# A fused causal conv and ELU MLP kernel: x loaded as fp32 and cast on chip, per-channel band weights, wide conv taps, w_out loaded earlier

## Chip, cores, metric

The kernel runs on one core of one Trainium2 chip. The metric is device time in microseconds (us), the median of a few executions. An execution of a one-core program counts as "fast" if it is within 1.5% of that kernel's fastest. A ratio is the mean time of one kernel's fast runs over the mean of the other's from the same rounds, so it is not quite the ratio of the medians that I quote.

The engines: PE is TensorE (matrix multiplies), DVE is VectorE, ACT is ScalarE, POOL is GpSimd, and SP is SyncE, which here only issues DMAs. DMAs that SP or ACT issue go through a hardware queue, those of GpSimd through the software queue. The granted clock is the share of its full speed at which PE is let run.

## The reference

```python
# x: (8, 4096, 192), weight: (8 heads, 7 taps), w_in: (192, 2048), w_out: (2048, 192)
w = softmax(weight, axis=-1)
out[b, s, h, :] = sum_k w[h, k] * x_pad[b, s + k, h, :]      # causal, 24 channels a head
h = out.reshape(32768, 192) @ w_in
g = where(h > 0, h, exp(min(h, 0)) - 1)
return g @ w_out                                             # float32
```

## The kernel before

The 32,768 tokens are handled in 32 super-tiles of 1,024. For each, a causal conv gives `att`, the first matmul with `w_in` gives 16 "pairs" of 2x512 columns in PSUM, ACT, POOL and DVE turn each pair into ELU values, and the matmuls with `w_out` follow one super-tile later. I number pairs from 0; pair 16 opens the second super-tile.

From the second super-tile on, the conv is a matmul with a banded matrix `Tm` that holds each head's 7 weights along a diagonal. `Tm` is made through DRAM by three DMAs that wait for each other: store zeros, write the diagonal over them, load the result. I call them the band chain: store, diagonal, reload.

```python
# SyncE (SP)
load_wd(sy, 0)                              # conv weights, one copy per channel
sy.dma_start(wq..., broadcast weight)       # all heads' weights on every partition
W(s_tz, 1); W(s_w[0], 32)                   # zeros ready; first part of w_in has landed
sy.dma_start(band[:, :, :], Tm[:, :, :]).then_inc(s_band, 16)          # store
W(s_band, 16); W(s_set, 5)                  # softmax of wq done
diagonal = bass.AP(tensor=band.tensor, offset=0,
                   ap=[[HEADS * TW + 1, P], [TW, HEADS], [1, KSIZE]])  # 128 x 8 x 7
sy.dma_start(diagonal, wprb[:]).then_inc(s_band, 16)                   # diagonal
W(s_band, 32)
sy.dma_start(Tm[:], band[:, :, :]).then_inc(s_band, 16)                # reload
```

The first super-tile cannot wait for that. Its conv uses x transposed on PE and small diagonal matrices `Dg` ("the early conv"), so that the w_in matmuls can start early. x comes as bf16 through GpSimd's software queue, which casts on the way; so do `w_in`, `w_out` and the later x tiles `xg`.

```python
# PE
warm(7)                                     # dummy matmuls of 512 columns
W(s_xl[0], 16); W(s_xl[1], 16)              # x has landed
# ... transposes, then 96 conv matmuls of 128 columns (48 pairs on two row groups)
# [cut] then in program order: pairs 0 to 6, banded conv, pairs 7 to 9, banded conv,
#       pairs 10 to 13, banded conv, pairs 14, 15, first w_out matmuls, pair 16 ...
if m == 0: W(s_band, 48)                    # the first banded conv waits for the band chain
elif n < NQ - 1: warm(2)                    # dummies between the first pairs
# GpSimd, ninth pair:  if n == W_OUT_AT (8): load w_out
```

Of the kernel before, what the change touches and what calls it, by code (L numbers as in the profile page):

```python
# [5 lines left out]
ALU = mybir.AluOpType  # L6
ACT = mybir.ActivationFunctionType
AXIS = mybir.AxisListType
# [21 lines left out]
LAG = -1  # L30
WCOLS = ((0, 512), (512, 1280), (1280, 2048))
Q_PART = (0,) * 4 + (1,) * 6 + (2,) * 6
WARM = (7, 2)
HALF_STEPS = (10, 10, 6, 6, 10, 11, 11)

CONV_AT = ((4, 1, 1), (12, 2, 0))
EARLY_CONV = {6: (1, 0), 9: (1, 1), 13: (2, 0)}
QUAD = 4
XTW = 136
HALO = 2  # L40
XW = 5
X_AT = ((5, 1), (10, 0), (13, 2))
W_OUT_AT = 8

PIECES = (
    ((0, 0, CW, 0), (1, 0, CW, CW), (2, 0, CW, 2 * CW), (3, 0, CW, 3 * CW), (4, 0, 24, 4 * CW)),
# [5 lines left out]
def bass_lightweight_conv__then__act_elu_kernel(  # L52
# [54 lines left out]
    for n in range(NP + NQ + LAG):  # L107
        s, i = divmod(n, NQ)
        if n < NP:
            slot_of_pair[n] = take_slot(("h", n))  # L110
            order.append(("h", n))
        if s == 0:
            convs = [EARLY_CONV[n]] if n in EARLY_CONV else []
        else:
            convs = [(s + ahead, g) for at, ahead, g in CONV_AT if at == i and n < NP]
        convs = [(k, g) for k, g in convs if k < NS]
        if n in rounds_at:
            t, half, r0, r1 = rounds_at[n]
            if (t, half) == last_half and r0 == 0:
                last_slot = take_slot(None)  # L120
            mid = (r0 + r1) // 2 if convs else r1
            order.append(("o", t, half, r0, mid))
            for k, g in convs:
                conv_at(k, g)
            if mid < r1:
                order.append(("o", t, half, mid, r1))
        else:
            for k, g in convs:
                conv_at(k, g)
# [5 lines left out]
    with ExitStack() as stack:  # L135
        def sbuf(name, shape, dt):
            return stack.enter_context(nc.sbuf_tensor(name, shape, dt))
# [4 lines left out]
        def sema(name):  # L142
            return stack.enter_context(nc.semaphore(name))
# [18 lines left out]
        E = sbuf("E", [P, NE, 2, GS], FP32)  # L162
        gT = sbuf("gT", [P, NG3, NQ, 2, GS], FP16)
        osb = sbuf("osb", [P, 2, 2, 2, D], FP32)
        wq = sbuf("wq", [P, HEADS, KSIZE], FP32)
        wmx = sbuf("wmx", [P, HEADS], FP32)
        wq2 = sbuf("wq2", [P, HEADS, KSIZE], FP32)
        wex = sbuf("wex", [P, HEADS, KSIZE], FP32)
        wsum = sbuf("wsum", [P, HEADS], FP32)
        wrs = sbuf("wrs", [P, HEADS], FP32)  # L170
        wprb = sbuf("wprb", [P, HEADS, KSIZE], BF16)
        zw = sbuf("zw", [P, GS], BF16)
        scr = sbuf("scr", [P, 2], FP32)
        H = psum("H", [P, 3, 2 * GS])
        ops = psum("ops", [P, 2, GS])

        s_wq = sema("s_wq")
        s_w = [sema(f"s_w{i}") for i in range(4)]
        s_wd = sema("s_wd")
        s_xl = [sema(f"s_xl{i}") for i in range(2)]  # L180
        s_id = sema("s_id")
        s_one = sema("s_one")
        s_z0 = sema("s_z0")
# [6 lines left out]
        s_hc = sema("s_hc")  # L190
        s_ha = sema("s_ha")
        s_hd = sema("s_hd")
        s_set = sema("s_set")
        s_wex = sema("s_wex")
        s_scr = sema("s_scr")
        s_x = [[sema(f"s_x{i}_{g}") for g in range(2)] for i in range(NXB)]
        s_od = sema("s_od")
# [86 lines left out]
        def _gpsimd(g: bass.BassGpSimd):  # L284
# [24 lines left out]
            def load_w_in(k):  # L309
                c0, c1 = WCOLS[k]  # L310
                for r in range(2):
                    g.dma_start(  # L312
                        w_in[HP * r : HP * (r + 1), :, c0:c1],
                        moe_w_in.rearrange("(p j) f -> p j f", j=3)[:, :, c0:c1],
                    ).then_inc(s_w[k], 16)

            def load_head(k):
                g.dma_start(
                    xh[:, k, :, :].rearrange("p i d -> p (i d)"),
                    x_flat[GS * k : GS * (k + 1), :].rearrange("(p i) d -> p (i d)", i=QUAD),  # L320
                ).then_inc(s_xl[k], 16)

            load_head(0)
            load_head(1)
            W(s_one, 1)
            g.affine_select(
                out=ident[:],
# [9 lines left out]
            for part in (1, 2):  # L337
                load_x(1, part)
            load_w_in(2)
            for n in range(NP):  # L340
                s, i = divmod(n, NQ)
                if n == W_OUT_AT:
                    g.dma_start(
                        w_out[:, :, :], moe_w_out.rearrange("(q p) d -> p q d", p=FC)
                    ).then_inc(s_w[3], 16)
                for at, part in X_AT:
                    if at == i and s + NXB < NS:
                        load_x(s + NXB, part)
                for u in range(2):
                    W(s_exp, 2 * n + u + 1)  # L350
                    g.tensor_scalar(  # L351
                        out=E[:, n % NE, u, :],
                        in0=E[:, n % NE, u, :],
                        scalar1=1.0,
                        scalar2=0.0,
                        op0=ALU.min,
                        op1=ALU.max,
                    ).then_inc(s_clp)

        @block.scalar  # L360
        def _scalar(a):
            W = Waits(a)
            load_wd(a, 1)
            a.memzero(scr[:, 0:1]).then_inc(s_scr)
            W(s_scr, 1)
            a.activation(scr[:, 1:2], scr[:, 0:1], ACT.Exp)
            W(s_v, 3)
            a.activation(wde[:], wd2[:], ACT.Exp, accum_out=wds[:]).then_inc(s_de)
            W(s_tp, 1)
# [16 lines left out]
            a.activation(  # L386
                att[:, 0, 2, 0 : GS // 2], H[:, 0, 0 : GS // 2], ACT.Copy
            ).then_inc(s_ha)
            W(s_set, 2)
            a.activation(wex[:], wq2[:], ACT.Exp).then_inc(s_wex)  # L390
            def evac(t, half):
                n_half = 2 * t + half
                W(s_mm2, n_half + 1)
# [42 lines left out]
        def _vector(v):  # L436
# [11 lines left out]
            v.tensor_scalar(  # L448
                out=wd2[:], in0=wd[:], scalar1=wdm[:, 0:1], scalar2=None, op0=ALU.subtract
            ).then_inc(s_v)  # L450
            W(s_de, 1)
            v.reciprocal(wdr[:], wds[:]).then_inc(s_v)
            W(s_v, 4)
# [5 lines left out]
                op0=ALU.mult,  # L459
                op1=ALU.mult,  # L460
            ).then_inc(s_D)
            W(s_tp, 3)
            v.tensor_copy(xT[:, 1, :, HALO : HALO + P], xt_bank(1)).then_inc(s_xtd)  # L463
            W(s_hc, 2)
# [1 line left out]
                att[:, 0, 1, :].rearrange("p (r t) -> p r t", r=2),  # L466
                H[:, 2, :].rearrange("p (r t) -> p r t", r=2)[:, :, 0 : GS // 2],
            ).then_inc(s_hd)
            W(s_wq, 16)
            v.tensor_reduce(wmx[:], wq[:], AXIS.X, ALU.max).then_inc(s_set)  # L470
            W(s_hc, 3)
            v.tensor_copy(
                att[:, 0, 2, GS // 2 : GS], H[:, 0, GS : GS + GS // 2]
            ).then_inc(s_hd)
            W(s_set, 1)
            v.tensor_tensor(
                wq2[:],
                wq[:],
                wmx[:, :].unsqueeze(2).to_broadcast([P, HEADS, KSIZE]),
                ALU.subtract,  # L480
            ).then_inc(s_set)
            W(s_wex, 1)
            v.tensor_reduce(wsum[:], wex[:], AXIS.X, ALU.add).then_inc(s_set)
            W(s_set, 3)
            v.reciprocal(wrs[:], wsum[:]).then_inc(s_set)
            W(s_set, 4)
            v.tensor_tensor(
                wprb[:, :, ::-1],
                wex[:],
                wrs[:, :].unsqueeze(2).to_broadcast([P, HEADS, KSIZE]),  # L490
                ALU.mult,
            ).then_inc(s_set)
            for n in range(NP):
                s, q = divmod(n, NQ)
                if s >= NG3:
# [20 lines left out]
        def _tensor(pe):  # L516
# [24 lines left out]

            warm(WARM[0])
            W(s_id, 1)
            W(s_xl[0], 16)
            W(s_xl[1], 16)
            for j in range(3):
                for i in range(QUAD):
                    ins = pe.matmul(  # L548
# [22 lines left out]
            for j in range(3):  # L571
                W(s_xta, (2, 2, 3)[j])
                if j:
                    W(s_xtd, 1)
                for k in range(KSIZE + 1):
                    for kb in range(2):
                        shift, i = divmod(2 * kb - PAD + k, QUAD)
                        for r in range(2):
                            ins = pe.matmul(  # L579
                                head_bank(j, r)[:, P * kb : P * (kb + 1)],  # L580
                                Dg[HP * r : HP * (r + 1), k : k + 2, :],
                                xT[HP * r : HP * (r + 1), j, i, HALO + shift : HALO + shift + P],
                                start=(k == 0 and kb == 0),
                                stop=(k == KSIZE),
                                tile_position=(HP * r, 0),
                                skip_group_check=True,
                            )
                ins.then_inc(s_hc)
            for item in order:
                if item[0] == "c":  # L590
# [79 lines left out]
        @block.sync  # L670
        def _sync(sy):
            W = Waits(sy)
            load_wd(sy, 0)
            sy.dma_start(
                wq[:, :, :].rearrange("p h k -> p (h k)"),
                bass.AP(tensor=weight.tensor, offset=0, ap=[[0, P], [1, HEADS * KSIZE]]),
            ).then_inc(s_wq, 16)
            W(s_tz, 1)
            W(s_w[0], 32)
            sy.dma_start(band[:, :, :], Tm[:, :, :]).then_inc(s_band, 16)  # L680
            W(s_band, 16)
            W(s_set, 5)
            diagonal = bass.AP(
                tensor=band.tensor,
                offset=0,
                ap=[[HEADS * TW + 1, P], [TW, HEADS], [1, KSIZE]],
            )
            sy.dma_start(diagonal, wprb[:]).then_inc(s_band, 16)
            W(s_band, 32)
            sy.dma_start(Tm[:], band[:, :, :]).then_inc(s_band, 16)  # L690

# [54 lines left out]
```

## Time and profile before

| | before |
|---|---|
| median | 759.63 us (758.85 to 760.06, 4 runs) |
| span of the profiled execution | 758.2 us |
| w_in matmuls begin (pair 0) | 15.42 us |
| first banded conv begins | 24.21 us |
| second super-tile begins (pair 16) | 43.27 us |

The windows view gives each engine's busy time in a stretch ("0.00:50.00 50.00" is the stretch and its length; PEclk is the granted clock).

```profile
core 0: us, PE busy (x) PEld busy (x) DVE busy (x) ACT busy (x) POOL busy (x), PEclk, DMA share, GB/s
0.00:50.00 50.00, 39.04 (x536) 19.32 (x539) 30.01 (x58) 29.69 (x56) 33.56 (x58) 1.00 0.69 114
50.00:100.00 50.00, 50.00 (x968) 35.04 (x958) 42.69 (x71) 44.72 (x80) 44.94 (x76) 1.00 0.45 96
```

From 50 us on PE is never free (further windows show the same up to 730 us); the only room is the head, the part before. So the start of pair 16 is the figure to follow: whatever moves it moves the end. The timeline of before (start, duration, engine, line, operation, and in brackets the idle time before it and what ended it):

```profile
8.42 0.61 PE L548 MATMUL H<-ident,xh 128*64 128x2 bf16 x9 [4.00 <-DMA xh<-in_x_dram]
...
10.83 0.34 SPq L680 DMA_DIRECT2D conv_band<-Tm  x1
...
15.42 0.82 PE L628 MATMUL H<-att,w_in 64*128 64x512 bf16 x6 [0.57 <-ACT att L386]
...
17.58 0.38 SPq L688 DMA_DIRECT2D conv_band<-wprb  x1
...
21.13 0.33 SPq L690 DMA_DIRECT2D Tm<-conv_band  x1
...
24.21 0.65 PE L604 MATMUL H<-Tm,xg 128*24 128x122 bf16 x40 [0.21 <-DVE gT L499]
...
43.27 0.82 PE L628 MATMUL H<-att,w_in 64*128 64x512 bf16 x6 [1.30 <-DMA att<-conv_slots]
```

A step of the band chain is issued when the one before it has landed, so the SPq lines give the chain's times: store 10.8 to 17.5, diagonal 17.6 to 21.1, reload 21.1 to about 24. The first conv waited for nothing of note: the band came just in time. Pair 16 waited 1.30 us for `att`.

### The profile page before, as it was taken

How to read it: one execution, taken by the hardware profiler on the slowest of the kernel's cores; microseconds unless marked ns; L12 is line 12 of the kernel's file. 1: busy time of each engine (PE TensorE's matmuls, PEld its weight loads, DVE VectorE, ACT ScalarE, POOL GpSimd, SP SyncE). 2: the span in 40 equal slices, each digit the busy share in tenths (PEclk: the TensorE clock that was granted, in tenths of full speed). 3: DMA queues.
4: the chain of work that ended last, by engine and by line, in shares of the span. 5: the costliest groups of instructions: out<-in, count | busy, mean ns of one | idle time of the engine just before them, and what ended most of it. 6: DMA issues, size and time to landing. Idle time of an engine off the chain costs nothing.

```text
span 758.2 us, 32332 instructions
## 1 busy us (share of the span) xinstructions
PE 742.6 (98%) x13911; PEld 513.4 (68%) x13911; DVE 636.8 (84%) x1043; ACT 646.9 (85%) x1161; POOL 660.6 (87%) x1107
## 2 busy tenths in 40 slices
PE   6889999999999999999999999999999999999997
PEld 4256676676767667667667667667667667667676
DVE  3778988988988988988988988988988988988993
ACT  3778888888888888888888888888888889889882
POOL 4879989989988988988988998988988998988892
PEclk9999999999999999999999999999999999999999
DMA  9643453443453453453453454354354354354112
GB/s 144 108 84 94 102 114 77 104 103 85 101 116 77 100 111 80 100 116 81 96 108 87 95 116 87 90 116 82 92 116 95 82 116 86 89 115 104 61 44 64
DMA packets 107135, 72.77 MB, mean 96 GB/s; under 512 B 44784, under 2 KB 106736, under 8 KB 106992
## 3 DMA queue, kind: packets, MB, share of 16 engines
q1 hardware_dynamic: 66344, 54.03, 23.6%
q0 software_dynamic: 40304, 16.47, 19.7%
q8 instruction: 109, 1.79, 1.0%
q14 instruction: 34, 0.28, 0.1%
q10 hardware_dynamic: 344, 0.20, 0.1%
HBM read 45.43 MB, written 41.71 MB: 115 GB/s over the span
## 4 chain that ended last, share of the span: by engine, by line
PE 95%; DMA 2%; ACT 1%; DVE 1%; POOL 1%; issue 0%; SPq 0%; POOLq 0%
PE H L628 44%; PE ops L657 44%; PE H L604 5%; DMA conv_slots<-csb 1%; DMA xh<-in_x_dram 1%; PE H L657 1%; DVE gT L499 0%; DMA att<-conv_slots 0%; PE ops L531 0%; ACT E L427 0%; PE H L579 0%; POOL E L351 0%; PE ops L579 0%; PE H L560 0%; SPq L279 0%
## 5 line engine op out<-in xcount | busy, mean ns | idle before, releaser
L499 DVE SCALAR_TENSOR_TENSOR gT<-E,H 128x512 f16<-128x512 f32 x1024 | 631.0, 682 | 98.4 <-POOL E L351 90.9
L351 POOL TENSOR_SCALAR E<-E 128x512 f32<-128x512 f32 x1024 | 604.0, 612 | 82.9 <-ACT E L427 79.3
L427 ACT ACTIVATE E<-H 128x512 f32<-128x512 f32 x1024 | 546.2, 605 | 87.4 <-PE H L628 73.8
L657 PEld LDWEIGHTS ops<-w_out,gT 64*128 64x128 f16 x8064 | 342.4, 94 | 109.6 <-ACT osb L405 10.9
L657 PE MATMUL ops<-w_out,gT 64*128 64x192 f16 x8064 | 414.4, 243 | 0.9 <-DVE gT L499 0.9
L628 PE MATMUL H<-att,w_in 64*128 64x512 bf16 x3072 | 407.3, 378 | 5.1 <-DVE gT L499 3.2
L628 PEld LDWEIGHTS H<-att,w_in 64*128 64x128 bf16 x3072 | 129.6, 94 | 107.2 <-DVE gT L499 6.0
L416 ACT ACTIVATE csb<-H 128x1024 bf16<-128x1024 f32 x62 | 63.5, 1024 | 0.0
L405 ACT ACTIVATE osb<-ops 128x768 f32<-128x768 f32 x63 | 51.6, 819 | 5.1 <-PE ops L657 5.1
L307 POOL DMA_DIRECT2D xg<-in_x_dram x62 | 52.2, 842 | 0.4 <-issue 0.4
L604 PE MATMUL H<-Tm,xg 128*24 128x122 bf16 (+1 forms) x2480 | 40.7, 209 | 0.7 <-DVE gT L499 0.7
L604 PEld LDWEIGHTS H<-Tm,xg 128*24 128x24 bf16 x2480 | 31.3, 92 | 11.3 <-issue 10.7
L531 PE MATMUL ops<-zw 128*128 128x512 bf16 x35 | 11.6, 434 | 1.2 <-DVE zw L438 1.2
L510 DVE COPY osb<-H 128x384 f32<-128x384 f32 x1 | 0.6, 558 | 8.9 <-PE H L657 8.9
L531 PEld LDWEIGHTS ops<-zw 128*128 128x128 bf16 x35 | 2.5, 106 | 7.5 <-issue 6.0
L657 PE MATMUL H<-w_out,gT 64*128 64x192 f16 x128 | 5.6, 243 | 0.1
L657 PEld LDWEIGHTS H<-w_out,gT 64*128 64x128 f16 x128 | 5.2, 94 | 0.3 <-PE H L657 0.3
L548 PE MATMUL H<-ident,xh 128*64 128x2 bf16 x12 | 0.8, 192 | 4.0 <-DMA xh<-in_x_dram 4.0
L397 ACT ACTIVATE osb<-H 128x384 f32<-128x384 f32 x1 | 0.5, 490 | 4.7 <-PE H L657 4.7
L548 PEld LDWEIGHTS H<-ident,xh 128*64 128x64 bf16 x12 | 0.7, 151 | 4.9 <-issue 4.9
L312 POOL DMA_DIRECT2D w_in<-in_moe_w_in_dram x6 | 3.8, 642 | 0.0
L463 DVE CAST xT<-H 128x512 bf16<-128x512 f32 x1 | 0.7, 692 | 3.5 <-PE H L560 3.5
(41 smaller groups left out, 26.4 us busy)
## 6 DMA issues: line engine op xcount, KB each, us to landing
out_dram<-osb SPq DMA_DIRECT2D x127, 192.0 KB, 2.7
conv_slots<-csb SPq DMA_DIRECT2D x62, 256.0 KB, 2.5
att<-conv_slots SPq DMA_DIRECT2D x186, 64.0 KB
xg<-in_x_dram POOLq DMA_DIRECT2D x31, 240.0 KB, 5.1
xg<-in_x_dram POOLq DMA_DIRECT2D x31, 192.0 KB, 4.4
w_in<-in_moe_w_in_dram POOLq DMA_DIRECT2D x4, 288.0 KB, 10.1
w_out<-in_moe_w_out_dram POOLq DMA_DIRECT2D x1, 768.0 KB, 9.9
xh<-in_x_dram POOLq DMA_DIRECT2D x2, 192.0 KB, 5.5
```

Of the source, the lines that this page charges most:

```text
L307: g.dma_start(xg[:, b, w0:w1, :], src).then_inc(s_x[b][part - 1], 16)
L312: g.dma_start(w_in[HP * r : HP * (r + 1), :, c0:c1], moe_w_in.rearrange("(p j) f -> p j f", j=3)[:, :, c0:c1],).then_inc(s_w[k], 16)
L351: g.tensor_scalar(out=E[:, n % NE, u, :], in0=E[:, n % NE, u, :], scalar1=1.0, scalar2=0.0, op0=ALU.min, op1=ALU.max,).then_inc(s_clp)
L405: a.activation(osb[:, b, :, :, :].rearrange("p g k d -> p g (k d)"), ops[:, :, 0 : 2 * D], ACT.Copy,).then_inc(s_oev)
L416: a.activation(csb[:, m % 4, :, :], H[:, slot_of_conv[m] % 3, :].rearrange("p (b t) -> p b t", b=2), ACT.Copy,).then_inc(s_ce)
L427: a.activation(E[:, n % NE, u, :], H[:, k, GS * u : GS * (u + 1)], ACT.Exp).then_inc(s_exp)
L499: v.scalar_tensor_tensor(out=gT[:, s % NG3, q, u, :], in0=E[:, n % NE, u, :], scalar=1.0, in1=H[:, slot_of_pair[n] % 3, GS * u : GS * (u + ...
L531: pe.matmul(ops[:, 0, :], zw[:, 0:P], zw[:], start=True, stop=True)
L548: ins = pe.matmul(halos()[HP:P, j, i, 0:HALO], xh[:, 0, i, j::3], ident[:, P - HALO : P], start=True, stop=True, tile_position=(0, HP),)
L604: ins = pe.matmul(H[SLOT * q : SLOT * q + CPH, k % 3, GS * hb + o : GS * hb + o + nc_], xg[:, s % NXB, w, CPH * h : CPH * (h + 1)], Tm[:, ...
L628: ins = pe.matmul(H[:, k % 3, GS * r : GS * (r + 1)], w_in[HP * r : HP * (r + 1), j, FC * q : FC * (q + 1)], att[HP * r : HP * (r + 1), s ...
L657: ins = pe.matmul(acc[:, g, D * kb : D * (kb + 1)], gT[HP * rt : HP * (rt + 1), t % NG3, q, g, t0 : t0 + P], w_out[HP * rt : HP * (rt + 1) ...
```

## The change

It is meant to start the head sooner. x arrives uncast through ACT's hardware queue and ACT and DVE cast it (both small loads of the conv weights now go out on SP; one was on ACT); eleven warm-ups instead of seven cover the wait; the early conv takes 256 columns at a time; the band's store waits for x only and its diagonal uses weights that exist per channel anyway; w_out is loaded at once; the third early banded conv moves behind pair 16.

```diff
-WARM = (7, 2)
+WARM = (11, 2)
-EARLY_CONV = {6: (1, 0), 9: (1, 1), 13: (2, 0)}
+EARLY_CONV = {6: (1, 0), 9: (1, 1), 16: (2, 0)}
 # GpSimd: the two casting loads of x are gone; w_out follows w_in directly
+            g.dma_start(w_out[:, :, :], ...)            # was: at the ninth pair
 # ACT: fp32 x in, half of it cast here
+            for k in range(2):
+                a.dma_start(xf[:, k, :, :]..., x_flat[GS * k : GS * (k + 1), :]...)
+            a.activation(xh[:, 0, :, :], xf[:, 0, :, :], ACT.Copy).then_inc(s_xha)
 # DVE: the other half, behind the per-channel softmax; the all-heads softmax is gone
             W(s_wd, 32)
             # ... max, subtract
+            W(s_xl[1], 16)
+            v.tensor_copy(xh[:, 1, :, :], xf[:, 1, :, :]).then_inc(s_xh)
+            v.tensor_scalar(out=wprb[:, ::-1], in0=wde[:], scalar1=wdr[:, 0:1], ...)
 # PE: 48 matmuls of 256 columns instead of 96 of 128   [cut]
 # SP
-            W(s_w[0], 32)
+            for r in range(2):
+                W(s_xl[r], 16)
             sy.dma_start(band[:, :, :], Tm[:, :, :]).then_inc(s_band, 16)
             W(s_band, 16)
-            sy.dma_start(diagonal, wprb[:])             # rows (128), heads (8), taps
+            W(s_wp, 1)
+            sy.dma_start(                               # heads (8), rows (128), taps
+                bass.AP(tensor=band.tensor, offset=0,
+                        ap=[[TW, HEADS], [HEADS * TW + 1, P], [1, KSIZE]]),
+                wprb[0:HP:8, :].unsqueeze(1).to_broadcast([HEADS, P, KSIZE]),
+            ).then_inc(s_band, 16)
```

More of the change, by code (lines that the diff above doesn't have):

```diff
@@ L42 @@
 X_AT = ((5, 1), (10, 0), (13, 2))
-W_OUT_AT = 8
 PIECES = (
@@ L111, in bass_lightweight_conv__then__act_elu_kernel @@
             order.append(("h", n))
-        if s == 0:
-            convs = [EARLY_CONV[n]] if n in EARLY_CONV else []
-        else:
-            convs = [(s + ahead, g) for at, ahead, g in CONV_AT if at == i and n < NP]
+        convs = [EARLY_CONV[n]] if n in EARLY_CONV else []
+        if s:
+            convs += [(s + ahead, g) for at, ahead, g in CONV_AT if at == i and n < NP]
         convs = [(k, g) for k, g in convs if k < NS]
@@ L164, in bass_lightweight_conv__then__act_elu_kernel @@
         osb = sbuf("osb", [P, 2, 2, 2, D], FP32)
-        wq = sbuf("wq", [P, HEADS, KSIZE], FP32)
-        wmx = sbuf("wmx", [P, HEADS], FP32)
-        wq2 = sbuf("wq2", [P, HEADS, KSIZE], FP32)
-        wex = sbuf("wex", [P, HEADS, KSIZE], FP32)
-        wsum = sbuf("wsum", [P, HEADS], FP32)
-        wrs = sbuf("wrs", [P, HEADS], FP32)
-        wprb = sbuf("wprb", [P, HEADS, KSIZE], BF16)
+        wprb = sbuf("wprb", [P, KSIZE], BF16)
+        xf = sbuf("xf", [P, 2, QUAD, D], FP32)
         zw = sbuf("zw", [P, GS], BF16)
@@ L175, in bass_lightweight_conv__then__act_elu_kernel @@
         ops = psum("ops", [P, 2, GS])
-        s_wq = sema("s_wq")
         s_w = [sema(f"s_w{i}") for i in range(4)]
@@ L180, in bass_lightweight_conv__then__act_elu_kernel @@
         s_xl = [sema(f"s_xl{i}") for i in range(2)]
+        s_xh = sema("s_xh")
+        s_xha = sema("s_xha")
+        s_wp = sema("s_wp")
         s_id = sema("s_id")
@@ L192, in bass_lightweight_conv__then__act_elu_kernel @@
         s_hd = sema("s_hd")
-        s_set = sema("s_set")
-        s_wex = sema("s_wex")
         s_scr = sema("s_scr")
@@ L315, in load_w_in @@
                     ).then_inc(s_w[k], 16)
-            def load_head(k):
-                g.dma_start(
-                    xh[:, k, :, :].rearrange("p i d -> p (i d)"),
-                    x_flat[GS * k : GS * (k + 1), :].rearrange("(p i) d -> p (i d)", i=QUAD),
-                ).then_inc(s_xl[k], 16)
-            load_head(0)
-            load_head(1)
             W(s_one, 1)
@@ L339, in _gpsimd @@
             load_w_in(2)
+            g.dma_start(
+                w_out[:, :, :], moe_w_out.rearrange("(q p) d -> p q d", p=FC)
+            ).then_inc(s_w[3], 16)
             for n in range(NP):
                 s, i = divmod(n, NQ)
-                if n == W_OUT_AT:
-                    g.dma_start(
-                        w_out[:, :, :], moe_w_out.rearrange("(q p) d -> p q d", p=FC)
-                    ).then_inc(s_w[3], 16)
                 for at, part in X_AT:
@@ L362, in _scalar @@
             W = Waits(a)
-            load_wd(a, 1)
+            for k in range(2):
+                a.dma_start(
+                    xf[:, k, :, :].rearrange("p i d -> p (i d)"),
+                    x_flat[GS * k : GS * (k + 1), :].rearrange("(p i) d -> p (i d)", i=QUAD),
+                ).then_inc(s_xl[k], 16)
             a.memzero(scr[:, 0:1]).then_inc(s_scr)
@@ L366, in _scalar @@
             a.activation(scr[:, 1:2], scr[:, 0:1], ACT.Exp)
+            W(s_xl[0], 16)
+            a.activation(xh[:, 0, :, :], xf[:, 0, :, :], ACT.Copy).then_inc(s_xha)
             W(s_v, 3)
@@ L388, in _scalar @@
             ).then_inc(s_ha)
-            W(s_set, 2)
-            a.activation(wex[:], wq2[:], ACT.Exp).then_inc(s_wex)
             def evac(t, half):
@@ L461, in _vector @@
             ).then_inc(s_D)
+            v.tensor_scalar(
+                out=wprb[:, ::-1], in0=wde[:], scalar1=wdr[:, 0:1], scalar2=None, op0=ALU.mult
+            ).then_inc(s_wp)
             W(s_tp, 3)
@@ L468, in _vector @@
             ).then_inc(s_hd)
-            W(s_wq, 16)
-            v.tensor_reduce(wmx[:], wq[:], AXIS.X, ALU.max).then_inc(s_set)
             W(s_hc, 3)
@@ L474, in _vector @@
             ).then_inc(s_hd)
-            W(s_set, 1)
-            v.tensor_tensor(
-                wq2[:],
-                wq[:],
-                wmx[:, :].unsqueeze(2).to_broadcast([P, HEADS, KSIZE]),
-                ALU.subtract,
-            ).then_inc(s_set)
-            W(s_wex, 1)
-            v.tensor_reduce(wsum[:], wex[:], AXIS.X, ALU.add).then_inc(s_set)
-            W(s_set, 3)
-            v.reciprocal(wrs[:], wsum[:]).then_inc(s_set)
-            W(s_set, 4)
-            v.tensor_tensor(
-                wprb[:, :, ::-1],
-                wex[:],
-                wrs[:, :].unsqueeze(2).to_broadcast([P, HEADS, KSIZE]),
-                ALU.mult,
-            ).then_inc(s_set)
             for n in range(NP):
@@ L543, in _tensor @@
             W(s_id, 1)
-            W(s_xl[0], 16)
-            W(s_xl[1], 16)
+            W(s_xha, 1)
+            W(s_xh, 1)
             for j in range(3):
@@ L575, in _tensor @@
                 for k in range(KSIZE + 1):
-                    for kb in range(2):
-                        shift, i = divmod(2 * kb - PAD + k, QUAD)
-                        for r in range(2):
-                            ins = pe.matmul(
-                                head_bank(j, r)[:, P * kb : P * (kb + 1)],
-                                Dg[HP * r : HP * (r + 1), k : k + 2, :],
-                                xT[HP * r : HP * (r + 1), j, i, HALO + shift : HALO + shift + P],
-                                start=(k == 0 and kb == 0),
-                                stop=(k == KSIZE),
-                                tile_position=(HP * r, 0),
-                                skip_group_check=True,
-                            )
+                    shift, i = divmod(k - PAD, QUAD)
+                    step = 2 * XTW if i < 2 else 1 - 2 * XTW
+                    for r in range(2):
+                        whole = xT[HP * r : HP * (r + 1), j, i, HALO + shift : HALO + shift + P]
+                        ins = pe.matmul(
+                            head_bank(j, r),
+                            Dg[HP * r : HP * (r + 1), k : k + 2, :],
+                            bass.AP(
+                                tensor=whole.tensor,
+                                offset=whole.offset,
+                                ap=[whole.ap[0], [step, 2], [1, P]],
+                            ),
+                            start=(k == 0),
+                            stop=(k == KSIZE),
+                            tile_position=(HP * r, 0),
+                        )
                 ins.then_inc(s_hc)
@@ L672, in _sync @@
             W = Waits(sy)
-            load_wd(sy, 0)
-            sy.dma_start(
-                wq[:, :, :].rearrange("p h k -> p (h k)"),
-                bass.AP(tensor=weight.tensor, offset=0, ap=[[0, P], [1, HEADS * KSIZE]]),
-            ).then_inc(s_wq, 16)
+            for r in range(2):
+                load_wd(sy, r)
             W(s_tz, 1)
-            W(s_w[0], 32)
+            for r in range(2):
+                W(s_xl[r], 16)
             sy.dma_start(band[:, :, :], Tm[:, :, :]).then_inc(s_band, 16)
             W(s_band, 16)
-            W(s_set, 5)
-            diagonal = bass.AP(
-                tensor=band.tensor,
-                offset=0,
-                ap=[[HEADS * TW + 1, P], [TW, HEADS], [1, KSIZE]],
-            )
-            sy.dma_start(diagonal, wprb[:]).then_inc(s_band, 16)
+            W(s_wp, 1)
+            sy.dma_start(
+                bass.AP(
+                    tensor=band.tensor,
+                    offset=0,
+                    ap=[[TW, HEADS], [HEADS * TW + 1, P], [1, KSIZE]],
+                ),
+                wprb[0:HP:8, :].unsqueeze(1).to_broadcast([HEADS, P, KSIZE]),
+            ).then_inc(s_band, 16)
             W(s_band, 32)
```

## The prediction

> **What bounds the kernel now.** In the windows view PE is 100% busy from 50 to 730 us; the chain of waits is 95% PE. The change doesn't touch that steady part, only the head: PE waits for the bf16 x (4.0 us, landing at 8.3), runs slow, then is paced by DVE (0.68 us per half pair, about 1.29 us per pair). In the timeline the second super-tile's first matmul, where the steady part begins, is at 43.27. The change is worth what it moves that moment.
>
> **Steps.**
> 1. x. The casting load landed 6.3 us after issue. As fp32 from ACT (786 KB) I estimate landing at 4.5 and 5.5, from 2.5 to 2.7 us for 192 to 256 KB on hardware queues, plus casts of about 0.8 us (ACT moves 128x768 in 0.82). The Trainium skill, "DMA: Bandwidth & Descriptors", section "SWDGE vs HWDGE vs iDMA", ties casts during DMA to the GpSimd path; hence casts on chip. Both wd loads now follow each other on SP, and DVE's cast sits behind wd: transposes start near 7.0 instead of 8.42.
> 2. Warm-up and wide taps. The seven warm-up matmuls take 0.43 us each, later ones 0.27; the early conv (10.5 to 14.9) is slow for two thirds. With eleven, the gap before the transposes is about 1 us, and PE should be fast sooner. At full speed 24 wide pairs stream the columns of 48 narrow ones, so I give the width little, the warmth 1.5 us. First w_in matmul at about 12 instead of 15.42.
> 3. Band. The store waits for x, not w_in: issued near 6 (was 10.8, landed 17.5). Per-channel weights remove eight softmax steps (wprb was done at 16.5). The diagonal's slowest dimension becomes 8; by that page's section "Why a DMA increments its semaphore by 16 and not by 1" it runs on 8 engines: I allow 5 us instead of 3.5. The reload (2.7 us alone) now meets w_in and w_out traffic; a 256 KB store beside the w_out load took 6.8. I expect Tm near 21.5 instead of 24; the first conv, wanted near 20.5, waits about 1 us.
> 4. w_out earlier. Its issue (1.2 us on POOL at 28.9) delayed the clamps; its traffic stretched the second conv_slots store from about 3 to 6.84 us, so the second super-tile waited 1.3 us. Both go.
> 5. Third early conv later: about 0.9 us in the head, 0.6 us of PE in the steady part: 0.3 net.
>
> **Sum.** First conv at about 21.8; by the timeline's intervals the second super-tile starts about 14.5 us after it, at 36.3. Plus 0.6 for the moved conv: 36.9 against 43.27, a gain of about 6 us: some 2.5 through the first conv, the rest from 4 and 5.
>
> **Prediction: 753.7 us, range 751.0 to 757.0** (ratio 0.992). Faster by over 2%: 0.02; within 2%: 0.97; slower: 0.01.
>
> **What would show it.** Right: transposes near 7.0, first w_in matmul near 12, Tm landed 20 to 23.5, no clamp delayed by w_out, second super-tile at 35.5 to 38.5, a plain shift from there to the end. Wrong: a first conv at 24 or later; PE still slow through the early conv; the second super-tile waiting for att.
>
> **What would make it wrong.** Smaller gain (3 to 4): contention on the DMA rings holds the band back, and the earlier head only waits longer at the first conv. Larger (8): Tm by 20. A loss would need the fp32 x to land after 8.

## The result

| | before | changed |
|---|---|---|
| median | 759.63 us | 760.95 us (759.30 to 761.84, 4 runs) |
| ratio | | 1.0016, 95% interval 0.9997 to 1.0035: the same |
| span of the profiled execution | 758.2 | 760.1 |
| transposes begin | 8.42 | 7.92 |
| w_in matmuls begin | 15.42 | 14.62 |
| first banded conv begins (its wait) | 24.21 (0.21) | 27.60 (4.41) |
| pair 16 begins (its wait for att) | 43.27 (1.30) | 44.34 (none) |

The predicted gain of 6 us did not come; 753.7 was forecast, in a range that ended at 757.0. The timeline of the changed kernel:

```profile
6.01 0.36 SPq L655 DMA_DIRECT2D conv_band<-Tm  x1
...
7.92 0.53 PE L521 MATMUL H<-ident,xh 128*64 128x2 bf16 x9 [1.79 <-DVE xh L440]
...
13.74 0.64 SPq L658 DMA_DIRECT2D conv_band<-wprb  x1
...
14.62 0.82 PE L605 MATMUL H<-att,w_in 64*128 64x512 bf16 x6 [0.56 <-ACT att L376]
...
23.56 0.33 SPq L667 DMA_DIRECT2D Tm<-conv_band  x1
...
27.60 1.04 PE L581 MATMUL H<-Tm,xg 128*24 128x122 bf16 x40 [4.41 <-DMA Tm<-conv_band]
...
29.54 1.46 PE L605 MATMUL H<-att,w_in 64*128 64x512 bf16 x6
...
31.90 1.46 PE L605 MATMUL H<-att,w_in 64*128 64x512 bf16 x6
...
44.34 0.82 PE L605 MATMUL H<-att,w_in 64*128 64x512 bf16 x6 [0.41 <-DVE gT L472]
```

The store was issued 4.8 us sooner than before, yet the reload was issued 2.4 us later. The chain of waits, asked for the first 60 us, names the three DMAs (start, duration, what):

```profile
6.01 7.71 DMA conv_band<-Tm
...
13.74 9.81 DMA conv_band<-wprb
...
23.56 4.00 DMA Tm<-conv_band
```

By the same reading, from one issue to the next step, before needed 6.75, 3.55 and 3.1 us. The diagonal, 14 KB, took 9.8 us instead of 3.55. The reload's own packets passed only after 26 us: w_out's were through by 23, but those of the next xg load, which GpSimd issued at 22.47, passed from 24 to 27.

The second loss stands behind the wait. The windows view of the changed kernel, last columns PEclk, DMA share, GB/s:

```profile
9.63:14.06 4.43, 4.42 (x48) 3.42 (x48) 0.87 (x2) 0.95 (x2) 0.00 (x0) 0.62 1.29 215
13.88:27.50 13.62, 8.75 (x58) 2.20 (x54) 9.35 (x16) 7.98 (x15) 9.18 (x15) 0.97 1.13 151
27.50:34.36 6.86, 6.76 (x64) 2.03 (x64) 1.29 (x2) 3.07 (x5) 1.47 (x3) 0.56 0.17 54
34.36:50.00 15.64, 14.79 (x226) 7.01 (x224) 12.50 (x20) 12.91 (x24) 12.89 (x23) 1.00 0.29 67
50.00:100.00 50.00, 50.00 (x980) 35.15 (x978) 43.24 (x71) 44.35 (x80) 45.34 (x77) 1.00 0.42 95
```

Over nearly 7 us after the wait the mean granted clock is 0.56: six w_in matmuls take 1.46 us instead of 0.82, and pairs follow each other after 2.36 and 2.00 us instead of 1.29. The early conv, too, ran at 0.62. After 50 us PE is fully busy again, as before.

The wait that before had at pair 16 is gone, and still pair 16 begins 1.1 us later; the third conv behind it adds about 0.8 us more. That is the 1.9 us between the spans of these two executions.

### The profile page after: what moved, and what is told of

Same layout as the page of the kernel before. It is cut to its first block, busy times and chain, and to the rows that moved or that the text cites. A ratio compares the mean times of both kernels' runs of the same rounds, so it can differ in the third digit from the quotient of the medians.

```text
span 760.1 us, 32240 instructions
## 1 busy us (share of the span) xinstructions
PE 746.3 (98%) x13867; PEld 512.7 (67%) x13867; DVE 636.3 (84%) x1040; ACT 647.5 (85%) x1161; POOL 661.1 (87%) x1105
## 4 chain that ended last, share of the span: by engine, by line
PE 94%; DMA 3%; DVE 1%; POOL 1%; ACT 0%; issue 0%; ACTq 0%; SPq 0%
PE H L605 44%; PE ops L634 44%; PE H L581 5%; DMA conv_band<-wprb 1%; DMA conv_band<-Tm 1%; PE H L634 1%; DVE gT L472 1%; DMA xf<-in_x_dram 1%; DMA Tm<-conv_band 1%; POOL E L335 0%; PE ops L504 0%; ACT E L415 0%; POOL xg L300 0%; ACT osb L393 0%; DVE osb L483 0%
## 5 line engine op out<-in xcount | busy, mean ns | idle before, releaser
L404 ACT ACTIVATE csb<-H 128x1024 bf16<-128x1024 f32 x62 | 63.5, 1024 | 4.4 <-PE H L581 4.4
L504 PE MATMUL ops<-zw 128*128 128x512 bf16 x39 | 14.3, 480 | 1.2 <-DVE zw L426 1.2
L553 PE MATMUL H<-xT,Dg 64*128 64x256 bf16 x32 | 2.8, 339 | 0.0
```

The lines of the kernel that those rows point to most:

```text
L404: a.activation(csb[:, m % 4, :, :], H[:, slot_of_conv[m] % 3, :].rearrange("p (b t) -> p b t", b=2), ACT.Copy,).then_inc(s_ce)
L504: pe.matmul(ops[:, 0, :], zw[:, 0:P], zw[:], start=True, stop=True)
L553: ins = pe.matmul(head_bank(j, r), Dg[HP * r : HP * (r + 1), k : k + 2, :], bass.AP(tensor=whole.tensor, offset=whole.offset, ap=[whole.ap ...
```

## The experiments

My theory (A): the band chain bounds the head. Its hardware DMAs are held back by the software queue, which the change keeps busy until about 23 us (w_in, xg, then w_out), and the PE wait that results halves the clock. Rival (B): the new 8-headed form of the diagonal is slow in itself. Rival (C): the head is bounded by when the w_in matmuls begin. Eleven kernels ran; all gave correct results. Several are combinations that grew out of the ones before.

| run | first conv (wait) | pair 16 | median us | ratio to before, 95% interval |
|---|---|---|---|---|
| changed | 27.60 (4.41) | 44.34 | 760.95 | 1.0016, 0.9997 to 1.0035 |
| e1_wout_late | 22.99 (0.28) | 41.66 | 759.97 | 1.0006, 0.9989 to 1.0023 |
| e2_diag16 | 24.09 (0.92) | 38.49 | 756.79 | 0.9962, 0.9948 to 0.9977 |
| e3_before_diag8 | 24.50 (0.68) | 43.01 | 759.92 (1 run) | |
| e4_cast_first | 25.82 (5.04) | 41.83 | 759.36 | 0.9997, 0.9982 to 1.0012 |
| e5_store_early | 24.40 (1.80) | 40.21 | 757.72 | 0.9960, 0.9931 to 0.9989 |
| e6_store_cast | 24.59 (0.59) | 39.34 | 757.80 | 0.9966, 0.9936 to 0.9996 |
| e7_store_cast_diag16 | 23.83 (1.59) | 38.05 | 756.65 | 0.9953, 0.9929 to 0.9976 |
| e9_fill_wait | 26.52 (filled) | 40.73 | 758.54 | 0.9983, 0.9968 to 0.9998 |
| e10_diag_pool | 25.36 (3.95) | 41.99 | 758.32 | 0.9972, 0.9955 to 0.9988 |

By the rule of 2% all of these count as the same time as before; some intervals still exclude 1. Times of pair 16 come from one profiled execution each. They do set the time: span minus start of pair 16 is 714.9 us in the three kernels with the third conv ahead of it (before, e3, e11) and 715.7 to 716.1 us in the ten others. But the runs of one kernel spread by 1 to 4 us, and if the rest is as constant as that, the spread lies in the head: a difference of 1 or 2 us between two single executions proves little, and the changed kernel's profile is the slowest of its four runs. What carries the theories is therefore how long the single DMAs took, and whether that repeats. Only before and e3 in this table have the third conv ahead of pair 16, so add about 0.8 us to the others when comparing them with these two (pairs 16 and 17 lie 1.49 us apart in before and 2.30 in the changed kernel). For example, e1's 41.66 is worth about 42.5 against 43.27, and its interval allows that or nothing.

### e1_wout_late: w_out back at the ninth pair

```diff
-            g.dma_start(w_out[:, :, :], ...)            # right after w_in
+                if n == W_OUT_AT:                       # 8
+                    g.dma_start(w_out[:, :, :], ...)
```

> The changed kernel with w_out's load put back to the ninth pair; all else as changed. In the changed kernel the diagonal took 9.8 us from issue (13.7) to landing (23.5), the reload landed at 27.6. Theory A (the software queue's traffic holds the band's hardware DMAs back): the software queue has 786 KB less to move, about 4 us, so it is empty near 19.5; the diagonal lands at 19.5 to 21, the reload at 22.5 to 24, the first conv's wait shrinks from 4.4 to under 1 us and the PE clock is not halved after it. The second super-tile then starts at 40 to 42.5 (44.34 changed, 43.27 before), the time is 756 to 759. Theory B (the diagonal is slow because it runs on 8 engines, whatever else runs): it still lands near 22.5 to 23.5, the first conv starts near 27, the time stays near 761.

The timeline of this run, the diagonal's and the reload's issue, the first conv and pair 16:

```profile
13.79 0.64 SPq L660 DMA_DIRECT2D conv_band<-wprb  x1
...
20.16 0.33 SPq L669 DMA_DIRECT2D Tm<-conv_band  x1
...
22.99 0.65 PE L583 MATMUL H<-Tm,xg 128*24 128x122 bf16 x40 [0.28 <-DMA Tm<-conv_band]
...
41.66 0.82 PE L607 MATMUL H<-att,w_in 64*128 64x512 bf16 x6 [2.79 <-DMA att<-conv_slots]
```

The same diagonal, issued at the same time, took 6.4 us instead of 9.8; the reload 2.8 instead of 4.0; the wait at the first conv fell from 4.41 to 0.28. The 9.8 is no chance: e4, e8 and e9 below keep this diagonal beside the early w_out, and there it took 9.9, 9.0 and 9.1 us. That is A, and against B. Pair 16 came where A had it (40 to 42.5), but the time, 759.97, did not (756 to 759), and pair 16 could have come sooner: the late load brought back the wait there, 2.79 us. So the early w_out is right for pair 16 and wrong for the band: the change had moved the contention from one chain to another.

### e3_before_diag8: the new form in the quiet place

The kernel before, with only the diagonal's write in the new form.

```diff
-            diagonal = bass.AP(..., ap=[[HEADS * TW + 1, P], [TW, HEADS], [1, KSIZE]])
-            sy.dma_start(diagonal, wprb[:]).then_inc(s_band, 16)
+            W(s_wp, 1)
+            sy.dma_start(bass.AP(..., ap=[[TW, HEADS], [HEADS * TW + 1, P], [1, KSIZE]]),
+                wpd[0:HP:8, :].unsqueeze(1).to_broadcast([HEADS, P, KSIZE])).then_inc(s_band, 16)
```

> The kernel before with only the diagonal's write changed to the 8-head form with per-channel weights (the old softmax still runs, its result unused). The store still lands at 17.5, when the software queue has under 3 us of work left, so this measures the 8-engine form almost alone: before it took 3.5 us from issue to landing. Theory A: 4 to 5 us, first conv at 24.5 to 26. Theory B: 8 us or more, first conv at 28 or later.

Its timeline, the diagonal's and the reload's issue:

```profile
17.50 0.64 SPq L689 DMA_DIRECT2D conv_band<-wpd  x1
...
21.76 0.32 SPq L698 DMA_DIRECT2D Tm<-conv_band  x1
```

That is 4.3 us against 3.55, in one execution. B predicted 8 or more and is refuted as a cause by itself.

### e2_diag16: the old form in the busy place

```diff
-                    ap=[[TW, HEADS], [HEADS * TW + 1, P], [1, KSIZE]],
-                wprb[0:HP:8, :].unsqueeze(1).to_broadcast([HEADS, P, KSIZE]),
+                    ap=[[HEADS * TW + 1, P], [TW, HEADS], [1, KSIZE]],
+                wpr8[:],      # all heads' softmax on every partition, computed early
```

> The changed kernel with the diagonal written over 128 rows again (weights of all heads on every partition, as before, but computed early), w_out still early. Theory B: the diagonal lands 3.5 to 5 us after its issue at 13.7, so near 18, Tm near 22, no wait at the first conv, time 755 to 757.5. Theory A: the first packets still come only some 4 us after issue (near 18), but 64 packets per engine instead of 128 interleave with the software queue in half the time, 2.5 instead of 5 us: it lands near 21, Tm near 25, first conv waits about 2 us, time 758 to 760.

```profile
13.13 0.37 SPq L690 DMA_DIRECT2D conv_band<-wpr  x1
...
20.78 0.33 SPq L699 DMA_DIRECT2D Tm<-conv_band  x1
...
24.09 0.65 PE L609 MATMUL H<-Tm,xg 128*24 128x122 bf16 x40 [0.92 <-DMA Tm<-conv_band]
...
38.49 0.82 PE L633 MATMUL H<-att,w_in 64*128 64x512 bf16 x6 [0.41 <-DVE gT L500]
```

The diagonal took 7.65 us. It landed at 20.8, as A expected (21), not at 18 (B); but the first conv came 1 us sooner than A's 25, because the reload was quicker. The time, 756.8, was better than A's 758 to 760 and inside B's 755 to 757.5, so here the DMA's landing speaks for A and the time does not. With this one change of a write's shape the changed kernel ends 0.4% ahead of before; the clock, too, stayed whole after a wait of 0.9 us.

How a 14 KB write can take that long is seen in the DMA view: packets of the hardware queue (q1, only the diagonal here) and of the software queue (q0) in two busy microseconds, columns packets, MB, share of 16 engines (the packets' times added up, so it can pass 100%). Before, from 18.5 to 20.5 us:

```profile
q1 hardware_dynamic: 1040, 0.01, 26.9%
q0 software_dynamic: 47, 0.06, 16.3%
```

The changed kernel, from 19 to 21 us:

```profile
q0 software_dynamic: 961, 0.37, 150.6%
q1 hardware_dynamic: 463, 0.01, 33.7%
```

e2, from 17 to 19 us:

```profile
q0 software_dynamic: 690, 0.35, 126.2%
q1 hardware_dynamic: 690, 0.01, 46.9%
```

e1, from 17 to 19 us:

```profile
q1 hardware_dynamic: 997, 0.01, 29.7%
q0 software_dynamic: 49, 0.06, 17.8%
```

The diagonal is some thousand writes of 14 bytes (8 heads x 128 rows), each a packet of its own on this queue. With the other queue nearly idle they pass in 2 us, in either form (before and e1). Beside a full software queue they take turns with it: in e2 exactly one for one (and in e7, from 17 to 18 us, 294 for 295). In the changed kernel it is one for two. The Trainium skill, "DMA: Bandwidth & Descriptors", section "Queues, rings and completion order", says each engine "round-robins between the queue rows it has work for, at *packet* granularity"; and by its section "Why a DMA increments its semaphore by 16 and not by 1" the slowest dimension sets how many engines a DMA uses, here 8 against 16. Both fit the counts: on 8 of 16 engines a write can only meet half of the software packets (961 / 2 = 480, against 463). An estimate from these numbers: 961 software packets in 2 us on 16 engines are 30 per us and engine, so 128 writes per engine need about 4.3 us; the slices show the diagonal's packets from 17.6 to 23.3. The number of engines is inferred from these ratios; the view does not list engines.

Most of the rest of the 9.8 us is the time before the first packet. It is about 1 us in before (issue at 17.58, packets from 18.5 on) and nearly 4 us in the changed kernel (issue at 13.74, no q1 packet between 14 and 17.5). It is 3 us in e1, too (issue at 13.79, packets from 16.8 to 19), where w_out is out of the way but w_in and xg still fill the queue until 17. So the early w_out explains the longer passing of the packets, some 5.5 us instead of 2, and not the late start. Why the start is as late as that is not settled.

### e4_cast_first: earlier w_in matmuls

```diff
+            W(s_xl[1], 16)
+            v.tensor_copy(xh[:, 1, :, :], xf[:, 1, :, :]).then_inc(s_xh)
             W(s_wd, 32)                                  # was above the cast
```

> The changed kernel with the DVE's cast of x placed ahead of the per-channel softmax, so that it does not wait for the weights (landed 6.9). Transposes start near 6.6 instead of 7.9, PE idles 0.5 us instead of 1.8, and if the halved clock from 10.5 to 13.9 came from that idle time the early conv takes about 2.8 us instead of 4.4 and the first w_in matmul comes at 11.5 to 12.5 instead of 14.6. If the band chain bounds the head (my theory), the first conv still starts at 27 to 28 and the time stays within 1 us of the changed kernel's 761. A rival (the head is bounded by when the w_in matmuls begin) expects 758 to 759.

```profile
8.83:11.65 2.82, 2.81 (x48) 2.53 (x48) 1.13 (x3) 0.94 (x2) 0.19 (x1) 1.00 1.10 199
```

This is the windows view of the early conv: 2.82 us at clock 1.00, against 4.43 at 0.62 in the changed kernel. The w_in matmuls began at 12.21, 2.4 us sooner, and PE then waited longer at the first conv, 5.04 us. That is the band chain as the bound, and against C. Two of my figures were off. The first conv came at 25.82, not 27 to 28: the diagonal was issued 0.9 us sooner, because the store took 6.4 us instead of 7.7 (I do not know why), and the reload took 3.1 us instead of 4.0. The reload may owe that to the earlier matmuls: GpSimd issued the next xg load at 20.05 instead of 22.47, so its packets were through sooner, and e8 (19.65, reload 2.9) and e9 (21.81, reload at most 3.9) fit that; no run isolates it. And the median, 759.36, is not within 1 us of the changed kernel's but 1.6 below it and 0.4 above what C expected. The two come from different rounds and their intervals overlap: a small gain is possible, 2.4 us is not seen in the medians.

### e8_narrow_cast: the width of the taps

e4 with the 96 matmuls of 128 columns of before.

```diff
-                            head_bank(j, r), ..., [step, 2], [1, P]     # 256 columns
+                    for kb in range(2):
+                                head_bank(j, r)[:, P * kb : P * (kb + 1)], ...
```

> The changed kernel with the cast of x first (full clock in the early conv, which then took 2.8 us with 24 wide pairs) and the conv taps narrow again, 48 pairs of 128 columns. The prediction gave the width little: at full clock 2.6 to 3.2 us. If the width is what shortens the early conv it takes 3.8 or more. The first conv waits for the band either way, so the time does not move.

The early conv took 2.87 us (8.37 to 11.24) at clock 1.00, against 2.82 with wide taps; the single time was 759.33. At full clock the width is worth nothing that these two executions show: it saves instructions, not columns.

### e9_fill_wait: the cost of the halved clock

```diff
                     if m == 0:
+                        warm(18)
                         W(s_band, 48)
```

> The changed kernel with 18 more dummy matmuls of 512 columns ahead of the first conv (18 x 0.22 us, about 4 us), in the place where PE waits 4.4 us for the band; nothing else. The band still lands near 27.5. If the idle wait is what halves the PE clock afterwards (27.5 to 34.4 in the changed kernel, where two pairs took 2.36 and 2.0 us instead of 1.29 and the conv 1.04 instead of 0.65), the clock stays full and the second super-tile starts near 42 instead of 44.34, time 758 to 759.5. If the stall costs only its own length, it starts at 44 to 45 and the time stays near 761.

```profile
26.52 0.65 PE L582 MATMUL H<-Tm,xg 128*24 128x122 bf16 x40
...
40.73 0.82 PE L606 MATMUL H<-att,w_in 64*128 64x512 bf16 x6 [0.41 <-DVE gT L472]
```

The dummies change no data that anyone reads, yet the clock (third figure from the end) stayed at 1.00 in the windows view:

```profile
22.50:40.00 17.50, 16.69 (x185) 6.29 (x188) 11.01 (x19) 12.04 (x21) 11.80 (x21) 1.00 0.41 88
```

Pair 16 came 14.2 us after the first conv, against 16.7 in the changed kernel: the idle wait costs 2.5 us after it is over. (In this execution the band itself came 1.1 us sooner, so the 3.6 us of pair 16 are not all due to the fill.) The time, 758.5, is inside what I wrote.

### e5, e6, e7: the store sent early

```diff
             W(s_tz, 1)
-            for r in range(2):
-                W(s_xl[r], 16)
             sy.dma_start(band[:, :, :], Tm[:, :, :]).then_inc(s_band, 16)
```

e5 is this alone, e6 adds e4's order of the cast, e7 adds e2's diagonal to both.

> The changed kernel with the band's zero store no longer waiting for x: it goes out right after the two weight loads, near 2.3 us, before the software queue's packets (from 5 us). If hardware DMAs are slow to start only beside the software queue, its first packet comes 2 us after issue and it lands by 6 to 7 instead of 13.7, at a cost of up to 0.8 us to x. The diagonal is then issued when its weights are ready, near 9.5, still beside the software queue: first packet 4 to 5 us later, but mostly ahead of w_out's packets (17 to 23 us), landing 16 to 18; reload landed 20.5 to 23, first conv then or when wanted (23 to 24). Second super-tile 38 to 40, time 756 to 758. If instead a DMA of this chain costs what it costs whatever runs beside it (store 7.7 us), it lands at 10, the diagonal at 20, the reload at 24.

> The early zero store together with the DVE's cast of x ahead of the softmax. The cast alone moved the w_in matmuls to 12.2 and gained nothing at the first conv but waiting (5.0 us). With the band ready near 21 both gains count: first conv wanted at 20.5 to 21.5 and started by 22, clock full throughout, second super-tile at 36 to 37.5, time 754 to 756.

> As the last, with the diagonal over 128 rows (16-way). Its weights are ready later (near 11 instead of 9), so if the diagonal now runs ahead of w_out's packets the 16-way form has nothing left to gain and the later issue costs up to 1.5 us: first conv 21.5 to 23.5, time within 1 us of the last kernel's, not better. If the 8-way form is the cost everywhere, this one is 2 to 3 us faster than the last.

In e5 the diagonal went out at 9.11 instead of 13.74. The view of SP's waits shows what it cost there (line, what it waited for, us):

```profile
SPq L665 <- DMA conv_band<-wprb: 11.9, 1, 11.9
```

So 4.6 us gained at its issue became 1.9 at its landing (21.7 instead of 23.6). e6's diagonal, issued at 9.76, landed at 21.8. My expectation, landing at 16 to 18 ahead of w_out, was wrong. I read it so: while the software queue's packets are larger, its turns are longer. From 13 to 20 us in e5 it moved 2,382 packets and 1.35 MB, 567 bytes each, against 385 bytes each in the changed kernel's window above, and in those 7 us 986 packets of q1 got through. The gain that e5 does show comes with a shorter wait (1.80 instead of 4.41) and a smaller loss of clock (pair 16 follows the first conv after 15.8 us instead of 16.7).

In e6's execution the cast did not even help: transposes began at 8.08, since the second half of x landed only near 7.4. The early store beside x is not shown to be the cause: e7, e10 and e11 have the same store and cast, and there DVE's cast of that half began between 5.8 and 6.2. With the clock whole from 15 us on, pair 16 followed 14.75 us after the first conv. e7 ended within noise of e2 and 1.1 us ahead of e6, between my two expectations. e2 and e7 beat before (ratios 0.9962 and 0.9953, both intervals below 1) and lie below the changed kernel's ratio, too, in intervals that do not overlap.

### e10_diag_pool: the diagonal inside the software queue

e6, with the diagonal issued from GpSimd ahead of w_out.

```diff
+            W(s_band, 16); W(s_wp, 1)                    # on GpSimd
+            g.dma_start(bass.AP(..., ap=[[TW, HEADS], [HEADS * TW + 1, P], [1, KSIZE]]),
+                wprb[0:HP:8, :].unsqueeze(1).to_broadcast([HEADS, P, KSIZE])).then_inc(s_dg, 16)
             g.dma_start(w_out[:, :, :], ...)
```

> Early zero store and early cast, with the 8-way diagonal issued from the software queue itself, ahead of w_out (the casting loads before it are then served first, w_out after). In the two runs with an early store the diagonal was issued at 9.1 and 9.8 on a hardware queue, beside the software queue, and landed at 21.7 and 21.8, whatever its issue. If what holds it back is that its 1024 small writes take turns with another queue's packets, in the same queue they run in 2 to 3 us after w_in's last packets (near 17.5): landing 18 to 20, Tm 21 to 23, first conv with less than 1 us of waiting, time 755 to 757. If the small writes are slow beside any traffic, landing 21 or later and no gain over the early-store run with the early cast (757.8).

From the list of DMA issues (KB each, us from issue to landing):

```profile
conv_band<-wprb POOLq DMA_DIRECT2D x1, 14.0 KB, 12.1
```

and from the timeline the first conv:

```profile
25.36 1.04 PE L592 MATMUL H<-Tm,xg 128*24 128x122 bf16 x40 [3.95 <-DMA Tm<-conv_band]
```

It landed at 21.0, at my limit for "no gain". The view holds a surprise: in the software queue the 1,024 writes went as only 48 packets (5,200 software packets up to 40 us, against 5,152 in the changed kernel, e4 and e8, which make the same loads), and still the diagonal landed only 0.7 us sooner than e6's 1,024 packets did. So the number of packets is not the whole price of such a write. How much of the 12.1 us it waited behind w_in and xg is not shown. And w_out, issued 2.0 us later than in e6, was then beside the reload, which took 4.3 us. No gain over e6.

### e11_third_conv_13: the third conv

e7 with `EARLY_CONV = {6: (1, 0), 9: (1, 1), 13: (2, 0)}`.

> The kernel with early store, early cast and 16-way diagonal (second super-tile at 38.05, third early conv after it, at 39.24), with the third early conv put back after the fourteenth pair. The prediction costed the move at 0.9 us in the head against 0.6 us in the steady part, net 0.3. So the second super-tile starts at 38.7 to 39.1, and a few pairs later the kernel is 0.1 to 0.5 us behind the other; the time does not tell them apart.

Pair 16 began at 39.89, 1.84 us later than in e7, and the pairs after 17 were 0.92 later (pair 21 at 47.38 against 46.46). The first conv of this execution was itself 0.45 later. So the move is worth about 1.4 us in the head and costs about 0.9 behind pair 16, or 1.1 counted to the end of the span: net 0.3 to 0.5, where I had 0.3. The single time, 756.90, does not tell them apart.

## Why the prediction was wrong

**The step that failed is step 3**, "I expect Tm near 21.5 instead of 24; the first conv, wanted near 20.5, waits about 1 us". Tm came at 27.6 and the first conv waited 4.4 us. Its terms: the store was issued when I said, near 6. The diagonal was allowed 5 us and took 9.8; that one term is 4.8 of the 6.1 us by which Tm was late. With 5 for the diagonal, 21.5 leaves 10.5 us for store and reload together; they took 7.7 and 4.0, about 1.2 more. I had listed the cause myself ("contention on the DMA rings holds the band back") but sized the diagonal from before's 3.5 us, measured when the software queue was nearly empty, and from its engines. Beside a full queue its packets took some 5.5 us to pass instead of 2, and the first came nearly 4 us after issue instead of 1. e1 (less traffic: 6.4 us) and e2 (the 16-way form: 7.65 us) each brought most of the wait down; e3 shows that the form alone costs 0.7 us. Why the first packet comes so late stays open.

**The second missing term is the clock.** My "14.5 us after it" for pair 16 was right wherever the clock stayed whole (14.2 in e9 and e7, 14.4 in e2, 14.75 in e6). In the changed kernel it was 16.7, and 16.0 to 16.6 in e4, e8 and e10, which also waited 4 to 5 us. So of the 8.0 us by which pair 16 missed my 36.3, 5.8 are the first conv and 2.2 the clock behind it.

**Step 1** was nearly right in kind, 0.9 us short in size: the transposes began at 7.92 instead of 7.0. The weights landed at 6.9 beside x, and DVE's cast stood behind them (e4).

**Step 2** failed: the w_in matmuls began at 14.62, not 12. The warmth did not last through the early conv (0.62). e4 shows both that 2.8 us is what a warm early conv takes and that it would not have helped the time, since the band came later still. That the width is worth little was right (e8).

**Step 4** was right: pair 16 no longer waited for att, and e1 brings the wait back (2.79 us). **Step 5** was right as far as one execution of e11 tells: 0.3 to 0.5, where I had 0.3.

**The bound** was read rightly: the steady part did not change, and all but the third conv's 0.8 us happened before pair 16. The forecast class, within 2%, held; the time, 760.95, lay outside the range.

Open: why a hardware DMA's first packet comes 3 us or more after issue beside a full software queue; why the store took 1.3 us less in e4; why the diagonal was not quicker as 48 packets in e10; and how much idle time it takes to lose the clock.

## What to carry to other kernels

A DMA of many tiny writes is not priced by its bytes: on the hardware queue 14 KB passed in 2 us while the other queue was nearly idle and took about 3.5 to 7.5 us beside a queue of large casting loads, not counting its late start; in e2 the 16-way form took 7.65 us from issue to landing where the 8-way form took 9.0 to 9.9. Before you move a load earlier, look at which chain of dependent DMAs it will then run beside; here the early w_out freed one chain and blocked another. And an idle wait on PE can cost more than its length: 4.4 us of waiting cost 2.5 us more in clock, and dummy matmuls in the gap saved that (e9).

## What the Trainium skill lacked or had wrong

- "DMA: Bandwidth & Descriptors", "Queues, rings and completion order": the turn-taking is there and the runs agree (690 packets against 690). What it means for a DMA of tiny packets beside another queue is not spelled out: 2 us of transfer became about 5.5 (8-way) or 3.5 (16-way) in the changed kernel and e2. It also gives 9 to 17 descriptors as typical for a packet; on the hardware queue here each 14-byte write was counted as a packet (1,040 in 2 us, about the 1,024 writes), and on the software queue the same writes made 48 packets, some 21 writes each (e10).
- The same page, "Latency and other measured facts", gives about 600 ns to the first byte on a hardware queue. Before shows about 1 us with the other queue nearly idle; the changed kernel nearly 4 us beside a full software queue. The page has no figure for a first byte beside another queue that is full.
- "TensorE: Matmul & The Clock Gate", the table "Why this matters for your kernels", warns of idle gaps of more than about 3 us. Here a gap of 1.79 us before the transposes was followed by a clock of 0.62 in the early conv (changed kernel), a gap of 0.99 was not (e4), and one of 0.76 with another of 0.72 after the transposes was (e7, 0.62). At the first conv a gap of 1.80 us was followed by slow pairs (e5: 1.45 us instead of 0.82), one of 1.84 was not (e11). So a gap's length alone does not decide; the page's free-running window (Part 1) may be why, but no run here sets its phase.
- The same page warns in Part 1 that clock events in traces have been seen to be unreliable on trn2. No page that I used says that the profile can show a clock of 1.00 where the matmuls run slow: before's first warm-ups take 0.43 us each under a clock shown as 1.00, and the same matmuls take about 0.23 in e9's fill; before's early conv takes 4.4 us under 1.00, e4's 2.8. So early in a span the durations decide, not the clock shown.
